# A new issue order for the first five eighths of a one-core attention-and-MoE kernel: same instructions, other places, some on other engines

## The chip, the cores and the metric

The kernel runs on one core of one Trainium2 chip. Such a core has five engines that each take their instructions strictly in order: PE (TensorE, matmuls, with its weight loads shown as PEld), DVE (VectorE), ACT (ScalarE), POOL (GpSimd) and SP (SyncE), which here only issues DMAs. Engines wait for each other by semaphores. The metric is the time of one execution on the device in microseconds (us). For the kernel before, three runs gave 907.27, 907.62 and 909.55 us, median 907.62.

## The reference, cut to what matters

Batch 4, 8 heads, 768 positions, 64 values a head; then a gated feed-forward layer over 3072 tokens, 512 wide, 1536 inside.

```python
q_bucket = sum((q @ proj > 0) * 2**arange(6)); k_bucket likewise
mask = q_bucket[:, :, :, None] == k_bucket[:, :, None, :]
scores = where(mask, q @ k.T / sqrt(64), -1e9)
attn = exp(scores - max);  attn = attn / (sum(attn) + 1e-09)
x = (attn @ v), heads side by side          # 3072 x 512
return ((x @ w_a) * (x @ w_b)) @ w_out      # all in float32
```

## The kernel before

**Tiling.** A batch is cut into 3 chunks of 256 tokens, a chunk's attention into 2 halves of 4 heads, a half into 8 score tiles of 128 queries by 768 keys. So there are 192 score tiles. A tile is named by batch, chunk, half, head pair in the half, head in the pair and token tile: `e_1_2_0_0_1_1` is the exponential of batch 1, chunk 2, half 0, pair 0, head 1, tile 1.

**One score tile** (`qtile`, L1044). PE computes `s` (L1056, with keys `kTA`, `kTB` and queries `qTA`, `qTB`, each transposed, of 16-bit parts and bucket marks). DVE takes the row maximum `mx` (L1070) and a small `width` (L1079); `bias` runs on ACT (L1086) or DVE (L1092). ACT makes `e`, the exponential (L1102). `e` is split into a 16-bit high part (a cast into `a2`, on DVE L1113, ACT L1114 or POOL L1115) and a low part (a subtraction on POOL L1125 or DVE L1129). SP issues a DMA transpose of both, `at` (L1135), and PE multiplies it with the values `vh` and `vl` into `av` (L1144). The first chunk of batch 0 goes another way, by PE transposes (`et`, L1023, and `av`, L1037).

**The feed-forward part** (`moe`, L1325) of a chunk has 12 steps f. PE makes `ab` (L1349, 24 matmuls), ACT scales one half into `a` (L1363), DVE multiplies into `g` (L1371), `g` is split into 16-bit parts (L1379 on ACT or L1383 on DVE; L1391 on POOL), and PE adds `o` (L1401, 6 matmuls). There is one PSUM buffer for `ab`: the `ab` of step f+1 begins only when the `g` of step f has read it. So `a` and `g` stand between each two `ab`.

**Preparing a batch.** For each of the 4 head pairs of a batch SP loads keys (`rk_k`, L737) and values (`vr`, L737), and for each chunk queries (`rq_q`, L952). The first reader of such a load is an absolute maximum or sum: on ACT L754, on DVE L757 (`mx_k`, `mx_v`), for queries L962 or L968. Then come a PE broadcast `ps` (L463), `al` (L469), the scale, the split into the parts `nB` (L886, L890, L907), copies into `marked` (L898, L902), a DMA transpose (L847), the bucket matmuls `b_k`, `b_q` (L819) and their marks (L828, L832). The weights of the feed-forward part are loaded and split during batch 0 (L532 to L665).

**What sets the order.** Every operation is recorded first (`Plan.op`), with the engine it runs on by default and, for the free pieces, with one or two other engines (`alt`). `Plan.issue` then walks over the table `ORDER` (L104 to L300): an entry is the number of an operation, plus 10000 or 20000 where its first or second other engine is taken; a negative entry -n puts n matmuls named `warm` (L1505) on PE, which compute nothing that is used. So the table alone sets what stands behind what on each engine, DMA issues on SP included.

```python
for x in order:
    if x < 0:
        fill(-x)
        continue
    which, at = divmod(x, 10000)
    o = self.ops[at]
    (o.alt[which - 1][2] if which else o.fn)()
```

Of the kernel before, what the change touches and what calls it, by code (L numbers as in the profile page):

```python
# [75 lines left out]
def constants():  # L76
# [28 lines left out]
    2, 7, 1, 4, 6, 13, 5, 0, 53, 61, 41, 8, 280, 254, 276, 10014, 3, 9, 281, 10, 277, 11, 15, 10054, 27, 12, 257,  # L105
    16, 10062, 138, 17, 55, 258, 56, 57, 253, 63, 10018, 42, 64, 19, 65, 59, 43, 20, 44, 256, 21, 392, 67, 46, 391,
    10022, 278, -5, 47, 282, 10295, 283, 23, 10048, 24, 279, -6, 25, 284, 290, 60, 285, 286, 45, 26, 287, 288, 68,
    289, -13, 49, 50, 10028, 291, -6, 51, 294, 259, 10267, 322, 52, 323, 296, 10139, 260, 10272, -13, 29, 326, 255,
    150, 30, 327, 261, 31, -9, 140, 262, 70, 141, 32, 263, 69, 264, 78, 71, 266, 33, 10406, 72, 79, 271, 10073, 80,
    265, 74, 34, 81, -20, 86, 268, 82, 396, 75, 395, 87, 94, 20269, 300, 76, 299, 142, 270, 88, 83, 143, 95, 84,  # L110
    328, 96, 324, 89, 97, -7, 85, 10336, 90, 325, 329, 98, 393, 91, 330, 145, 331, 92, 35, 394, 146, 99, 10151, 273,
    100, 559, 397, 20274, 10036, 304, -7, 152, 398, 303, 153, 275, 332, 399, 154, -7, 400, 37, 401, 155, 333, 38,
    335, 402, -6, 39, 157, 405, 93, 10040, 144, 158, 292, 337, 102, 110, 410, 103, 293, 147, 148, 560, 104, 149,
    10105, 403, 106, 111, 20297, 340, 561, 162, 10318, -16, 107, 112, 306, 368, 118, 113, 305, 313, 10341, 302, 301,
    108, 156, 119, 114, -11, 159, 77, 407, 562, 126, 120, 307, 160, 121, 408, 564, 122, 163, 409, 565, 411, -15,
    308, 115, 309, 127, 101, 116, 161, 128, 179, 310, 129, 342, 317, 123, 412, 130, 373, 180, 134, -9, 187, 20413,
    312, 178, 117, 188, 298, 124, 170, 189, 311, 190, -5, 131, 181, 191, 314, 182, 132, 195, 414, 375, 345, 109,
    183, 196, 133, 315, 334, 184, 197, 10198, 203, 319, 185, 199, 316, 58, 204, 192, 350, 349, 10171, 205, 566,
    10193, 346, 206, 369, 567, 207, 20320, 372, 172, 173, 211, 135, 569, 321, 404, 174, 164, 125, 165, 176, 219,
    166, 646, 168, 200, 136, 20338, 212, 201, 194, 563, 213, 364, 10214, 202, 169, 568, 208, 215, 339, 220, 186,  # L120
    209, 227, 221, 10222, 351, 216, 223, 228, 10359, 210, 217, 235, 229, 230, 177, 224, 231, 819, 10382, 236, 225,
    570, 237, 370, 20343, 232, 10238, 571, 239, 218, 344, 371, 233, 579, 572, 10573, 137, 574, 226, 580, 234, 243,
    575, 581, 588, 10820, 582, 240, 576, 583, 589, 241, 597, 244, 590, 20584, 821, 577, 591, 242, 598, 592, 585,
    599, 245, 600, 606, 601, 374, 20593, 586, 607, 822, -4, 615, 594, 608, 66, 246, 578, 609, 10602, 616, 610, 595,
    603, 247, 10611, -10, 624, 617, 824, 604, 618, 619, 249, 625, 825, 620, -10, 633, 376, 626, 248, 347, 627, 628,
    348, 612, -4, 250, 634, 10629, 377, 596, 635, 378, 10636, 621, 352, 647, 637, 613, 353, 379, 648, 251, 354, 587,
    630, 355, 605, 10638, 649, 622, 10650, 356, 656, 651, 252, 639, 631, 363, 657, -3, 665, 464, 20652, 358, 658,
    10659, 175, 666, 653, 614, 660, 667, 465, 10668, 640, 357, 669, 360, 674, 466, 381, 623, 10823, 467, 683, 654,
    365, 468, 471, 661, 469, 684, 419, 10670, 472, 662, 420, 675, 361, 415, 685, 416, 641, 676, 10686, 473, 10362,
    470, 677, 663, 687, 10671, 678, 826, 632, 474, 20366, 386, 827, 478, 383, 828, 387, 479, 10367, 475, 642, 692,  # L130
    476, 480, 643, 644, 10679, 701, 481, 477, 688, 388, 439, 384, 485, 689, 693, 672, 482, 430, 694, 10695, 486,
    702, 444, 483, 696, 418, 680, 664, 703, 487, 492, 655, 10704, 697, 829, 488, 710, 385, 705, 422, 681, 495, 711,
    489, 435, 443, 712, 496, 10713, 417, 440, 698, 714, 1103, 380, 484, 690, 421, 389, 167, 490, 423, 441, 424, 497,
    830, 390, 425, 10706, 426, 673, 498, 429, 831, 839, 502, 840, 499, 707, 434, 832, 841, 682, 10833, 446, 699,
    834, 503, 500, 427, 10842, 428, 715, 843, 491, 431, 708, 504, 716, 505, 848, 432, 445, 509, 442, 459, 433, 447,
    849, 448, 510, 506, 493, 449, 450, 719, 850, 10494, 857, 851, 507, 511, 523, 691, 835, 436, 501, 717, 852,
    10836, 508, 844, 1079, 20437, 512, 1104, 858, 709, 845, 10853, 866, 859, 1105, 837, 645, 700, 1106, 516, 10860,
    10438, 846, 861, 517, 1108, 513, 454, 514, 867, 875, 1109, 518, 854, 718, 10862, 519, 515, 868, 876, 869, 453,
    863, 720, 855, 877, 527, 721, 520, 10878, 870, 722, 526, 521, 723, 879, 1107, 838, 871, 906, 455, 884, 864,
    11080, 1110, 522, 872, 528, 1111, 456, 529, 1112, 847, 885, 530, 457, 880, 1081, 533, 886, 1082, 10887, 1083,  # L140
# [1403 lines left out]
```

## Time and profile before

| what | value |
|---|---|
| median of three runs | 907.62 us (907.27 to 909.55) |
| the profiled execution | 907.48 us, of which 905.4 us from first to last instruction |
| PE busy, share of the span | 865.2 us, 96% |
| DVE, ACT, POOL busy | 660.1, 539.9, 437.5 us |
| mean granted TensorE clock | 0.997 of full speed |
| DMA queue q1, share of 16 engines' span | 80.2% |

The profiled execution stands 2.08 us above its span and 0.14 us below the median of the runs. Busy PE time includes the `warm` matmuls. In the rows a name's numbers are left out, so `rk_k` is each of the key loads; which one it is follows from the order of the instructions.

### The profile page before, as it was taken

The page shows a single profiled execution, that of the slowest core. Times are in us where ns is not written, and L with a number is a line of the kernel's source. Part 1 is how long each engine was busy: PE and PEld are TensorE (multiplying, and loading weights), DVE is VectorE, ACT ScalarE, POOL GpSimd, SP SyncE. Part 2 cuts the span into 40 slices and gives each one's busy share as a digit, 9 for nine tenths or more (in the row PEclk, how much of TensorE's full clock was granted, in tenths as well). Part 3 has the DMA queues.
Part 4 walks back from the last instruction along what each step waited for, and adds up shares of the span by engine and source line. Part 5 has one row for each costly group of instructions (what it writes and reads, how often), then busy time and mean ns, then how long its engine had stood idle before and what let it go on. Part 6 is the DMA issues. An engine that isn't in the chain of part 4 may idle for free.

```text
span 905.4 us, 23135 instructions
## 1 busy us (share of the span) xinstructions
PE 865.2 (96%) x9252; PEld 661.0 (73%) x9252; DVE 660.1 (73%) x1557; ACT 539.9 (60%) x1043; POOL 437.5 (48%) x384
## 2 busy tenths in 40 slices
PE   4799899999999998999999999999999999999998
PEld 3678687776777776777777777777777777777775
DVE  6999999988778787779767667767888865652210
ACT  6897899967655665465653466545666655452212
POOL 1568868685544454353543264564454544362111
PEclk9999999999999999999999999999999999999999
DMA  8786699999988899989759679998899966744000
GB/s 315 253 225 188 125 238 241 180 194 192 210 179 143 158 175 181 160 168 171 148 126 165 106 151 157 191 173 150 152 188 164 174 110 105 130 94 72 1 24 24
DMA packets 416987, 142.61 MB, mean 158 GB/s; under 512 B 388592, under 2 KB 409200, under 8 KB 416880
## 3 DMA queue, kind: packets, MB, share of 16 engines
q1 hardware_dynamic: 416880, 141.14, 80.2%
q8 instruction: 72, 1.18, 0.5%
q14 instruction: 35, 0.29, 0.1%
HBM read 37.82 MB, written 6.29 MB: 49 GB/s over the span
## 4 chain that ended last, share of the span: by engine, by line
PE 70%; DVE 15%; DMA 6%; ACT 3%; issue 3%; SPq 2%; POOL 1%; ACTq 0%; DVEq 0%; POOLq 0%
PE ab L1349 34%; PE o L1401 16%; PE s L1056 10%; PE av L1144 7%; DMA at<-a 3%; DVE mx L1070 3%; PE av L1037 2%; DMA rq_q<-in_q_dram 1%; ACT e L1102 1%; DVE g L1371 1%; DVE wmx L637 1%; DVE nB_q L907 1%; DMA rk_k<-in_k_dram 1%; DVE wab L576 1%; DVE width L1079 1%
## 5 line engine op out<-in xcount | busy, mean ns | idle before, releaser
L1349 PE MATMUL ab<-xT,wab 128*128 128x256 f16 x3456 | 409.2, 273 | 7.5 <-DVE g L1371 7.3
L1349 PEld LDWEIGHTS <-wab 128*128 128x128 f16 x3456 | 333.5, 98 | 61.3 <-issue 8.9
L1125 POOL TENSOR_TENSOR a<-e,a 128x768 f16<-128x768 f32 x129 | 217.9, 1691 | 124.4 <-ACT a L1114 59.2
L1102 ACT ACTIVATE e<-s,bias,width 128x768 f32<-128x768 f32 x192 | 189.8, 989 | 82.3 <-DVE bias L1092 68.1
L1391 POOL TENSOR_TENSOR g<-g,g 128x256 f16<-128x256 f32 x144 | 103.7, 720 | 228.1 <-ACT g L1379 144.8
L1070 DVE TENSOR_REDUCE mx<-s 128x1 f32<-128x768 f32 x192 | 182.0, 950 | 38.9 <-PE s L1056 38.0
L1401 PE MATMUL o<-wo,g 128*128 128x512 f16 x864 | 209.0, 379 | 0.0
L1371 DVE SCALAR_TENSOR_TENSOR g<-ab,wlow,a 128x256 f32<-128x256 f32 x132 | 63.5, 481 | 105.6 <-ACT a L1363 98.2
L1401 PEld LDWEIGHTS <-g 128*128 128x128 f16 x864 | 81.3, 98 | 74.3
L1363 ACT ACTIVATE a<-ab,wcut 128x256 f32<-128x256 f32 x144 | 67.6, 469 | 110.3 <-PE ab L1349 108.4
L1144 PEld LDWEIGHTS <-at 128*128 128x128 f16 x3168 | 112.1, 98 | 22.3 <-DMA at<-a 4.6
L1144 PE MATMUL av<-vh,at 128*128 128x64 f16 x2112 | 115.4, 193 | 2.4 <-DMA at<-a 2.4
L1056 PE MATMUL s<-kTA_k,qTA_q 128*128 128x384 f16 x384 | 93.8, 326 | 5.6 <-ACT e L1102 3.5
L1056 PE MATMUL s<-kTB_k,qTB_q 128*128 128x384 f16 x384 | 93.8, 326 | 0.0
L1115 POOL CAST a<-e 128x768 f16<-128x768 f32 x52 | 44.5, 857 | 62.8 <-ACT e L1102 42.6
L1114 ACT CAST a<-e 128x768 f16<-128x768 f32 x83 | 68.6, 830 | 2.5 <-DMA at<-a 1.0
L1379 ACT CAST g<-g 128x256 f16<-128x256 f32 x103 | 41.4, 402 | 45.6 <-DVE g L1371 38.0
L1086 ACT ACTIVATE bias<-mx,width 128x1 f32<-128x1 f32 x91 | 26.4, 292 | 69.8 <-DVE width L1079 69.4
L1144 PE MATMUL av<-vl,at 128*128 128x64 f16 x1056 | 59.6, 193 | 0.0
L1056 PEld LDWEIGHTS <-qTB_q 128*128 128x128 f16 x384 | 37.5, 98 | 24.9
L1129 DVE TENSOR_TENSOR a<-e,a 128x768 f16<-128x768 f32 x47 | 47.0, 1002 | 8.4 <-ACT a L1114 6.6
L1056 PEld LDWEIGHTS <-qTA_q 128*128 128x128 f16 x384 | 34.8, 99 | 23.4 <-issue 5.9
(156 smaller groups left out, 871.7 us busy)
## 6 DMA issues: line engine op xcount, KB each, us to landing
rk_k<-in_k_dram SPq DMA_DIRECT2D x16, 384.0 KB, 4.4
vr<-in_v_dram SPq DMA_DIRECT2D x16, 384.0 KB, 4.3
rq_q<-in_q_dram SPq DMA_DIRECT2D x12, 512.0 KB, 4.7
raw_w<-in_moe_w_b_dram SPq DMA_DIRECT2D x12, 512.0 KB, 6.8
raw_w<-in_moe_w_a_dram SPq DMA_DIRECT2D x12, 512.0 KB, 6.4
raw_wo<-in_moe_w_out_dram SPq DMA_DIRECT2D x12, 512.0 KB, 5.7
out_dram<-ob SPq DMA_DIRECT2D x24, 256.0 KB, 2.8
at<-a SPq DMA_TRANSPOSE x176, 4.1
```

What stands on the lines that cost most here:

```text
L1056: nc.tensor.matmul(ps.t[:, jj, :HALF], lhsT=x.t[:, uq, :], rhs=y.t[:, h * NT + jj * 3 : h * NT + jj * 3 + 3, :].rearrange("p t x -> p (t x)"),
L1070: lambda: nc.vector.tensor_reduce(out=mx.t[:, u : u + 1], in_=halves(ps.t), axis=AX.XY, op=ALU.max, negate=True),
L1102: lambda: nc.scalar.activation(flat2(e.t), halves(ps.t), AF.Exp, bias=bias.t[:, u : u + 1], scale=width.t[:, u : u + 1], accum_out=sm.t[:, ...
L1114: ("ACT", 0.725, lambda: nc.scalar.copy(out=a2.t[:, 0], in_=e.t), False),
L1125: lambda: nc.gpsimd.tensor_tensor(out=a2.t[:, 1], in0=e.t, in1=a2.t[:, 0], op=ALU.subtract),
L1129: lambda: nc.vector.tensor_tensor(out=a2.t[:, 1], in0=e.t, in1=a2.t[:, 0], op=ALU.subtract), True,
L1144: nc.tensor.matmul(av.t[:, u, :], lhsT=at.t[:, a + kt, :], rhs=w.t[:, h, kt, :], start=i == 0, stop=i == 3 * NT - 1,)
L1349: nc.tensor.matmul(pl.t[:, m, :CH], lhsT=wt(m, wi, cc, f), rhs=xt.t[:, :, xi * NC + cc, :], start=i == 0, stop=i == 3 * NC - 1,)
L1363: lambda a=a, pl=pl, gr=gr: nc.scalar.activation(a.t, pl.t[:, 0, :CH], AF.Copy, scale=wcut[:, gr : gr + 1]),
L1371: lambda a=a, g32=g32, pl=pl, cut=cut: nc.vector.scalar_tensor_tensor(out=g32.t, in0=pl.t[:, 1, :CH], scalar=cut, in1=a.t, op0=ALU.mult, o ...
L1391: lambda g=g, g32=g32: nc.gpsimd.tensor_tensor(out=g[1].t, in0=g32.t, in1=g[0].t, op=ALU.subtract),
L1401: nc.tensor.matmul(po.t[:, u, :], lhsT=g[gi].t[:, us], rhs=wo[f // 2].t[:, f % 2, wi * DM : (wi + 1) * DM], start=f % per_q == 0 and i == ...
```

## The change

Only the table `ORDER` differs. Both tables hold the same 3658 operations. 198 of them run on another of their engines than before, and the negative entries (the `warm` matmuls) add up to 207 instead of 186. From the `ab` of batch 1, chunk 2, step 9 on, PE has the same sequence as before to the end; the other engines join within a few instructions of it. Over the whole program the casts of `e` are now 33 on DVE, 77 on ACT and 66 on POOL (41, 83 and 52 before). A line of the table from its start and one from the middle:

```diff
@@ -102,201 +102,201 @@
 ORDER = [
-    2, 7, 1, 4, 6, 13, 5, 0, 53, 61, 41, 8, 280, 254, 276, 10014, 3, 9, 281, 10, 277, 11, 15, 10054, 27, 12, 257,
...
-    1075, 11693, 11964, 1699, 1694, 1076, 1338, 1700, 1335, 1077, 1577, 21695, 1337, 1701, 1965, 1702, 1078, 1703,
...
+    2, 6, 7, 1, 5, 13, 4, 0, 53, 61, 41, 8, 254, 276, 281, 14, 9, 280, 10, 277, 15, 11, 10054, 258, 16, 257, 17, 27,
...
+    1964, 1939, 1719, 1337, 11720, 11077, 1335, 1721, 1965, 1569, 11966, 1339, 1336, 1706, 1340, 1580, 1968, 1341,
...
```

On DVE, in batch 1, chunk 2, ahead of the `g` of feed-forward step 5 of chunk 0 (`g_1_0_5`), these stood before; `rk_k2_1` is the key load of batch 2, pair 1:

```order
L907 SCALAR_TENSOR_TENSOR nB_k2_0_5758<-rk_k2_0_94,ks_k2_0_5940,nB_k2_0_5758 128x12x64
L1092 TENSOR_SCALAR bias_1_2_0_5524<-mx_1_2_0_5482,width_1_2_0_5519 128x1
L902 COPY marked_79<-nB_k2_0_5758 128x12x64
L757 TENSOR_REDUCE mx_k2_1_6034<-rk_k2_1_95 128x1
L1371 SCALAR_TENSOR_TENSOR g_1_0_5_6054<-ab_1_0_5_5967,wlow_76,a_1_0_5_6023 128x256
L1383 TENSOR_REDUCE g0_1_0_5_6060<-g_1_0_5_6054 128x256
```

Now these stand on DVE ahead of the same `g`:

```order
L1070 TENSOR_REDUCE mx_1_2_1_6008<-s_1_2_1_0_0_0_5981 128x1
L1079 TENSOR_SCALAR width_1_2_1_6025<-mx_1_2_1_6008,qsig_q1_2_4608 128x1
L1092 TENSOR_SCALAR bias_1_2_1_6027<-mx_1_2_1_6008,width_1_2_1_6025 128x1
L1070 TENSOR_REDUCE mx_1_2_1_6008<-s_1_2_1_0_0_1_6001 128x1
L1113 CAST a2_1_2_1_0_0_0_6065<-e_1_2_1_0_0_0_6030 128x768
L1079 TENSOR_SCALAR width_1_2_1_6025<-mx_1_2_1_6008,qsig_q1_2_4608 128x1
L1129 TENSOR_TENSOR a2_1_2_1_0_0_0_6065<-e_1_2_1_0_0_0_6030,a2_1_2_1_0_0_0_6065 128x768
L1371 SCALAR_TENSOR_TENSOR g_1_0_5_6080<-ab_1_0_5_6012,wlow_76,a_1_0_5_6075 128x256
```

The maximum over `rk_k2_1` has left DVE; it is now an L754 on ACT, behind `e_1_2_1_0_1_0`, and two score tiles of the next half have moved ahead of this `g`.

On ACT, a little earlier, the first reader of the key load of batch 2, pair 0 (`rk_k2_0`) stood like this, between the `a` of steps 2 and 3:

```order
L1363 ACTIVATE a_1_0_2_5706<-ab_1_0_2_5652,wcut_73 128x256
L1102 ACTIVATE e_1_2_0_0_1_1_5714,sm_1_2_0_5534<-s_1_2_0_0_1_1_5641,bias_1_2_0_5524,width_1_2_0_5519 128x768
L1379 CAST g0_1_0_2_5729<-g_1_0_2_5720 128x256
L1114 CAST a2_1_2_0_0_1_1_5732<-e_1_2_0_0_1_1_5714 128x768
L754 ACTIVATE nB_k2_0_5758,mx_k2_0_5759<-rk_k2_0_94 128x12x64
L1240 ACTIVATE xz_1_1_1_5778<-x_1_1_0_5276,xsc_1_1_5749 128x256
L1240 ACTIVATE xz_1_1_1_5778<-x_1_1_1_5716,xsc_1_1_5749 128x256
L1363 ACTIVATE a_1_0_3_5799<-ab_1_0_3_5734,wcut_73 128x256
```

And now, between the same two `a`:

```order
L1363 ACTIVATE a_1_0_2_5772<-ab_1_0_2_5695,wcut_73 128x256
L1379 CAST g0_1_0_2_5792<-g_1_0_2_5781 128x256
L1102 ACTIVATE e_1_2_0_1_0_1_5794,sm_1_2_0_5501<-s_1_2_0_1_0_1_5685,bias_1_2_0_5494,width_1_2_0_5492 128x768
L1086 ACTIVATE bias_1_2_0_5494<-mx_1_2_0_5478,width_1_2_0_5492 128x1
L1102 ACTIVATE e_1_2_0_1_1_0_5828,sm_1_2_0_5501<-s_1_2_0_1_1_0_5774,bias_1_2_0_5494,width_1_2_0_5492 128x768
L754 ACTIVATE nB_k2_0_5861,mx_k2_0_5862<-rk_k2_0_94 128x12x64
L1363 ACTIVATE a_1_0_3_5873<-ab_1_0_3_5799,wcut_73 128x256
```

The reader now stands behind the exponential of a tile three further on, with two exponentials and a bias between the `a` of step 2 and it; on SP the load's issue stands behind the transpose `at_1_2_0_0_0_0` as before and has moved ahead of the transpose `qTB_q2_0`.

On SP in batch 0, chunk 2, the key load of batch 1, pair 0 (`rk_k1_0`) stood like this:

```order
L1135 DMA_TRANSPOSE at_0_1_1_1_1_1_2260<-a2_0_1_1_1_1_1_2144 128x12x128
L737 DMA rk_k1_0_87<-in_k_dram 128x2x384
L1135 DMA_TRANSPOSE at_0_2_0_0_0_0_2313<-a2_0_2_0_0_0_0_2249 128x12x128
L1135 DMA_TRANSPOSE at_0_2_0_0_0_1_2351<-a2_0_2_0_0_0_1_2271 128x12x128
L847 DMA_TRANSPOSE qTB_q1_0_2379<-nB_q1_0_2278 128x16x128
L1135 DMA_TRANSPOSE at_0_2_0_0_1_0_2418<-a2_0_2_0_0_1_0_2301 128x12x128
```

And now:

```order
L1135 DMA_TRANSPOSE at_0_1_1_1_1_1_2250<-a2_0_1_1_1_1_1_2159 128x12x128
L1135 DMA_TRANSPOSE at_0_2_0_0_0_0_2317<-a2_0_2_0_0_0_0_2252 128x12x128
L1135 DMA_TRANSPOSE at_0_2_0_0_0_1_2370<-a2_0_2_0_0_0_1_2262 128x12x128
L847 DMA_TRANSPOSE qTB_q1_0_2394<-nB_q1_0_2272 128x16x128
L737 DMA rk_k1_0_87<-in_k_dram 128x2x384
L1135 DMA_TRANSPOSE at_0_2_0_0_1_0_2437<-a2_0_2_0_0_1_0_2344 128x12x128
```

The load has moved behind three transposes; its reader on ACT stands behind the same exponential, `e_0_2_0_1_0_1`, as before.

## Rows read from the trace of the kernel before

**Rows 1.** The page's first part: busy us, share of the span, instructions.

```profile
PE 865.2 (96%) x9252; PEld 661.0 (73%) x9252; DVE 660.1 (73%) x1557; ACT 539.9 (60%) x1043; POOL 437.5 (48%) x384
```

**Rows 2.** Windows: stretch, its us, each engine's busy us, clock, DMA share, GB/s.

```profile
20.00:112.00 92.00, 80.15 (x765) 65.98 (x764) 86.83 (x217) 78.98 (x125) 64.19 (x43) 1.00 0.74 204
112.00:200.00 88.00, 86.29 (x1015) 65.91 (x1015) 83.59 (x205) 80.49 (x145) 64.57 (x48) 1.00 1.12 214
200.00:507.60 307.60, 301.10 (x3304) 227.37 (x3302) 240.16 (x566) 173.62 (x356) 136.35 (x124) 0.99 0.90 166
507.60:880.00 372.40, 368.70 (x3960) 281.23 (x3959) 235.19 (x530) 189.23 (x393) 164.94 (x155) 1.00 0.72 127
```

**Rows 3.** Waits of PE: us in total, times, longest us.

```profile
PE ab L1349 <- DVE g L1371: 7.3, 7, 2.6
```

**Rows 4.** Timeline 340 to 350 us: start, us, engine, line, operation [idle before, releaser].

```profile
340.23 0.57 SPq L737 DMA_DIRECT2D rk_k<-in_k_dram  x1
...
341.15 2.78 PE L1349 MATMUL ab<-xT,wab 128*128 128x256 f16 x24
...
344.77 0.84 ACT L754 ACTIVATE nB_k<-rk_k 128x768 bf16<-128x768 f32 x1 [3.11 <-DMA rk_k<-in_k_dram]
...
346.41 0.45 ACT L1363 ACTIVATE a<-ab,wcut 128x256 f32<-128x256 f32 x1
...
346.97 0.48 DVE L1371 SCALAR_TENSOR_TENSOR g<-ab,wlow,a 128x256 f32<-128x256 f32 x1 [2.56 <-ACT a L1363]
...
347.51 1.47 PE L1349 MATMUL ab<-xT,wab 128*128 128x256 f16 x12 [1.36 <-DVE g L1371]
```

**Rows 5.** Timeline 357 to 364 us.

```profile
358.07 0.57 SPq L737 DMA_DIRECT2D rk_k<-in_k_dram  x1
...
361.82 0.95 DVE L757 TENSOR_REDUCE mx_k<-rk_k 128x1 f32<-128x768 f32 x1 [3.45 <-DMA rk_k<-in_k_dram]
362.69 0.47 DVE L1371 SCALAR_TENSOR_TENSOR g<-ab,wlow,a 128x256 f32<-128x256 f32 x1
```

**Rows 6.** Timeline of PE, 357 to 372 us.

```profile
363.22 4.45 PE L1349 MATMUL ab<-xT,wab 128*128 128x256 f16 x24 [2.55 <-DVE g L1371]
```

**Rows 7.** Windows, the ten us around that wait.

```profile
360.00:370.00 10.00, 7.45 (x72) 5.31 (x71) 5.65 (x11) 4.70 (x10) 4.37 (x5) 0.83 1.06 192
```

**Rows 8.** Timeline of PE, 192 to 196 us.

```profile
194.31 0.50 PE L1056 MATMUL s<-kTA_k,qTA_q 128*128 128x384 f16 x2 [1.17 <-DMA kTA_k<-marked]
```

**Rows 9.** Timeline 206 to 210 us.

```profile
206.99 1.64 POOL L1125 TENSOR_TENSOR a<-e,a 128x768 f16<-128x768 f32 x1
207.06 2.38 DVE L1129 TENSOR_TENSOR a<-e,a 128x768 f16<-128x768 f32 x1 [1.51 <-DMA rk_k<-in_k_dram]
...
208.39 0.35 PE L1144 MATMUL av<-vh,at 128*128 128x64 f16 x6 [0.83 <-DMA at<-a]
```

**Rows 10.** Timeline 488 to 500 us.

```profile
489.30 0.56 DVE L1113 CAST a<-e 128x768 f16<-128x768 f32 x1 [3.02 <-DMA at<-a]
...
497.91 2.34 PE L1349 MATMUL ab<-xT,wab 128*128 128x256 f16 x20 [0.78 <-DVE g L1371]
```

**Rows 11.** Timeline 150 to 164 us, SP and ACT.

```profile
150.71 0.57 SPq L737 DMA_DIRECT2D rk_k<-in_k_dram  x1
...
155.69 1.36 SPq L847 DMA_TRANSPOSE qTB_q<-nB_q  x1
...
161.40 0.84 ACT L754 ACTIVATE nB_k<-rk_k 128x768 bf16<-128x768 f32 x1 [0.43 <-DMA qTB_q<-nB_q]
```

**Rows 12.** Groups by line: busy us, mean ns of one, idle before.

```profile
L1129 DVE TENSOR_TENSOR a<-e,a 128x768 f16<-128x768 f32 x47 | 47.0, 1002 | 8.4 <-ACT a L1114 6.6 <-DMA rk_k<-in_k_dram 1.5
L1115 POOL CAST a<-e 128x768 f16<-128x768 f32 x52 | 44.5, 857 | 62.8 <-ACT e L1102 42.6 <-DMA at<-a 15.6 <-PE b_k L819 3.4
...
L1505 PE MATMUL warm<-ident 128*128 128x256 f16 x186 | 24.9, 281 | 0.0
```

**Rows 13.** Waits of DVE, 0 to 120 us: us in total, times, longest.

```profile
DVE mx L1070 <- PE s L1056: 2.3, 4, 0.9
DVE al_proj L469 <- PE ps_proj L463: 2.2, 1, 2.2
```

386 rows, old and new, of the table ORDER are left out of this document.

## The prediction

> **What bounds the kernel now.** I read the first part of the page, then busy time by stretches, then the waits of PE, and last the timeline around each wait. PE is busy for 865.2 of 905.4 us, 96%; DVE is next with 73% [rows 1]. So the end is set by PE: its busy time, plus the stretches where it stands. The difference between a stretch and PE's busy time in it tells where it stands [rows 2]: 11.85 us from 20 to 112, 1.71 from 112 to 200, 6.5 from 200 to 507.6, 3.7 from 507.6 to 880. The first 20 and the last 25.4 us hold the rest: 40.2 - 23.76 = 16.4. The `warm` matmuls are 24.9 us of the busy time [rows 12], and in the order all of them stand ahead of the first `ab` of batch 0, at some 112 us; so 20 to 112 us hold some 37 us in which PE has nothing useful to do, the largest reserve of this kernel.
>
> From batch 1, chunk 2, step 9 on, the edge of the stretches at 507.6 us, PE's sequence is unchanged, so whatever the change gains or loses has to happen before 507.6 us: in the start stage, or in the 1.71 + 6.5 = 8.2 us between 112 and 507.6. Most of these 8.2 us lie at six places, and I read what released PE at each.
>
> **Places that may be mended.** *First:* at 340.23 SP issues the key load of batch 2, pair 0; ACT stands 3.11 us for it and reads it only at 344.77, 4.54 us after the issue [rows 4]. The `a` of the feed-forward step is queued behind that reader, comes at 346.41, `g` at 346.97, and `ab` on PE begins at 347.51 after 1.36 us idle. In the changed order the reader stands behind an exponential three tiles further on, and the issue is a transpose earlier on SP. With tiles of 905.4 / 192 = 4.7 us, the reader gets several us more than the 3.11 it waited. I take the 1.36 as gone (bounds 0 and -1.36).
>
> *Second:* the load of pair 1 is issued at 358.07, and its reader, on DVE, waits 3.45 us and runs at 361.82; `g` stands directly behind it, at 362.69 [rows 5]. PE waits 2.55 us for it, and the `ab` behind that takes 4.45 us for 24 matmuls [rows 6], against 2.78 for the same 24 at 341.15 [rows 4]. The granted clock of 360 to 370 us is 0.83 [rows 7]: behind the 2.55 us of idle PE ran for a while at the lower level, 1.2 GHz, and that cost 4.45 - 2.78 = 1.67. The place is worth 2.55 + 1.67 = 4.22 us, the dearest of the middle. In the changed order the reader has left DVE and stands on ACT three tiles later. I take all 4.22 (bounds 0, where the late landing only meets ACT instead, and -4.22).
>
> *Third:* 1.17 us before the first `s` of batch 1 at 194.31, which waits for the transposed keys [rows 8]. In the changed order about 0.9 us more of PE's own work stands between the bucket matmuls of that pair and this `s`, by the groups of matmuls that the order lists there. I take -0.9 (0 to -1.17).
>
> *Fourth:* 0.83 us at 208.39, where `av` waits for `at` [rows 9]. The subtraction that makes its low part took 2.38 us on DVE against a mean of 1.00 for the line [rows 12], beside a POOL subtraction from 206.99. The reader of the key load of that place has moved from ACT to DVE, behind `g`; the landing may be covered or not. Half: -0.4 (0 to -0.83).
>
> *Fifth:* 0.78 us at 497.91 behind a cast on DVE that stood 3.02 us for the transpose that still read its buffer [rows 10]. The engines of the casts are shuffled there; -0.6 (0 to -0.78).
>
> Sum of what can be mended: -4.22 - 1.36 - 0.9 - 0.4 - 0.6 = -7.5, of the 8.2 us that are there.
>
> The fourth place is also where a rule speaks against the change. By the Trainium skill, "SBUF — State Buffer", section "Who interferes with whom", an instruction of DVE that reads two SBUF inputs and one of GpSimd exclude each other, since they share one port pair, for as long as an instruction lasts. The 2.38 us beside a POOL subtraction agree with it [rows 9]; the other runs of that line, 1.00 us in the mean [rows 12], with POOL busy in nearly half the span, don't show it as a steady cost. By the rule the 14 casts that move to POOL could hold up DVE; that is a rival below.
>
> **What the change adds.** *Spacing of `ab`.* `a` and `g` stand between two `ab`: from `a` at 346.41 to the next `ab` is 1.10 us [rows 4] at best. By the order, 25 places now have under 2 us of other PE work between two `ab` (16 before), the tightest one tile's `s` and `av`, about 1.2 us. The seven waits of `ab` for `g` sum to 7.3 us before, of which the three above are 4.69 [rows 3, 4, 6, 10]; the other 2.6 over 13 tight places are 0.2 each. Nine more places would then cost 1.8; some of them have DVE and ACT free ahead, so I take +0.85 (0 to 1.8).
>
> *The load of batch 1, pair 0* has moved behind three transposes on SP, the last of which, `qTB`, is issued 4.98 us later than the load was (155.69 against 150.71), while the reader stays behind the same exponential and ran at 161.40, after 0.43 us for the transpose's landing [rows 11]. Issued just behind it, at 157.05, and landing 4.54 us later as in [rows 4], the load is there at 161.6: 0.2 later than the reader ran before. I take +0.6, since the transposes share the DMA engines (bounds 0 and 4.22, the price of the worst such place).
>
> *The start.* DVE gets a `mx_k` (0.95 as in [rows 5]), two `bias` and a cast of 0.56 [rows 10] ahead of the first feed-forward inputs, and gives up a step of the split. The longest wait of DVE there is 2.2 us for one broadcast matmul, beside 2.3 in four small ones [rows 13]; the added work can fill that. I take +0.3; the bounds are -2.3 (all of the four waits gone) and +2.2 (a wait of the longest kind more).
>
> *21 more `warm` matmuls* cost nothing where they stand in waits, as nearly all do before 112 us; if all of them came on the path, 21 x 24.9 / 186 = 2.8 us [rows 12]. I take +0.4 (0 to 2.8).
>
> *New readers on DVE:* those of pairs 1 and 2 of batch 1 and pair 2 of batch 2, which were on ACT. Each runs 0.95 instead of 0.84, which is hidden with DVE at 240 of 307.6 us in that stretch [rows 2]. If its load is late, it holds the `g` behind it exactly as in [rows 5]: 0 to +4.22 each. I take 0: in the order all three stand one to three instructions behind a `g`, so that most of a feed-forward step lies before the next.
>
> Sum of the additions: 0.85 + 0.6 + 0.3 + 0.4 = +2.15. Together -7.5 + 2.15 = -5.3, and 907.48 - 5.3 = 902.2 us for an execution like the profiled one, which lies 0.14 under the median of the runs. So I predict 902.2.
>
> **The rivals.**
>
> *A, the idle time moves and does not go.* What removes a stall here lets PE run ahead until it meets the next late thing: more work of the same DVE (83.59 of 88.00 us busy from 112 to 200 [rows 2]) or another landing. There DVE, and not PE's own waits, sets the pace, and POOL's additional casts don't relieve it unless they are what DVE drops. For it: in that stretch DVE stands under 5%. Against: from 200 to 507.6 DVE has 67 us free, and the two dear places are single late landings, with no shortage of an engine behind them. By it only the clock loss and part of one gap go, -1.67 - 1.36 + 2.15 = about -0.9: 906.6. Chance 0.2.
>
> *B, a load lands late before a DVE reader.* The mechanism of [rows 5 to 7], now at two of the three readers that moved to DVE: the wait decides once it is longer than PE's work between the two `ab` (from 2 us on at many places), and a gap over 2.5 us brings the half clock with it. Price 2 x 4.22 = 8.4, on top of 902.2: 910.6, slower. For it: each of these readers is a first reader of a load, which is what DVE stood 3.45 us for. Against: on ACT these same readers stood in places without a gap on PE of that size, and DVE reaches them behind a `g`. Chance 0.11.
>
> *C, the casts on POOL block DVE.* 14 casts of 0.857 us [rows 12] that each hold up a two-input instruction of DVE on the path cost 12.0 us: 902.2 + 12.0 = 914.2. For it the 2.38 us of [rows 9]; against it the mean of 1.00 of that line. This is the rule of the Trainium skill named above, taken at its strongest. Chance 0.02.
>
> That the change doesn't do what it says is excluded: the readers and issues stand in other places in the order.
>
> **How the numbers follow.** The forecast has the remaining 0.67. Its own range is 898.5, where the starting stage gives 2.3 instead of costing 0.3 and the `ab` spacing costs nothing, to 904.9, where half of the 5.3 is not had. A difference under 0.3%, 2.7 us, can't be told from none: faster means under 904.9, slower over 910.3. The cases give faster 0.67, same 0.2, slower 0.13. The range leaves out B, C and a bit at the bottom: 898.5 to 908.5.
>
> **What would show it.** Right: the idle before the `ab` of batch 1, chunk 0, steps 4 and 6 is under 0.3 us, the granted clock of that ten us is 1.00, and the first feed-forward `ab` of batch 0 begins within a us of where it did. The first `s` of batch 1 waits under 0.4. Rival A: these gaps are gone, but PE's idle time from 112 to the joining place is still over 7 us, in other places. Rival B: a wait of over 2 us on DVE for a key load, a gap of PE behind it and a clock under 1 in that stretch. C: the mean of L1129 on DVE well over 1.00. Wrong altogether: a new stretch of PE idle that none of these names, above all before 112 us, where over 30 us are to be had or lost by changes that I priced at +0.3.

## The result and the profile after

The changed kernel takes 898.77 us (median of 4 runs, 897.19 to 900.57) against 907.44 us beside it: ratio 0.9903, 95% interval 0.9875 to 0.9932, faster by 8.7 us. Run once more with the experiments it took 898.19 us, ratio 0.9905 (0.9883 to 0.9926). Forecast were 902.2 and faster; the first median lies in the range (898.5 to 908.5) by 0.3 us, the second 0.3 us below it, and the gain is 1.6 times the forecast.

The first part of the page, answering to [rows 1] (busy us, share, instructions):

```profile
PE 863.4 (96%) x9273; PEld 662.1 (74%) x9273; DVE 644.3 (72%) x1544; ACT 535.1 (60%) x1040; POOL 448.2 (50%) x399
```

POOL has 10.7 us more to do, DVE 15.8 us less; PE is busy for 1.8 us less, so 8.2 of the 10.0 us that this execution's span is shorter are idle time of PE. The waits of PE, answering to [rows 3] (us in total, times, longest):

```profile
PE ab L1349 <- DVE g L1371: 2.3, 4, 0.8
...
PE s L1056 <- DMA qTA_q<-marked: 1.0, 1, 1.0
```

`ab` waits 2.3 us for `g` instead of 7.3, never over 0.8; a wait for the transposed queries has come. To see where, I cut the span at the starts of the same matmuls in each trace: the first `ab` of batch 0 chunk 0 (step 0), of batch 0 chunk 2 (step 6) and of batch 1 chunk 2 (step 9, the joining place), and of the last step of all. The rows are windows: stretch, its us, busy time of PE, PEld, DVE, ACT, POOL, clock, DMA share, GB/s. First the kernel before:

```profile
112.97:285.41 172.44, 169.66 (x1953) 128.79 (x1952) 150.25 (x376) 130.17 (x247) 105.51 (x85) 1.00 1.05 199
285.41:507.56 222.15, 217.04 (x2362) 164.07 (x2360) 172.48 (x394) 122.97 (x252) 94.40 (x87) 0.99 0.87 160
507.56:894.31 386.75, 383.05 (x4062) 291.22 (x4061) 237.11 (x534) 191.86 (x399) 167.66 (x159) 1.00 0.70 122
```

The kernel before in a second trace, taken with the experiments:

```profile
113.28:285.61 172.33, 169.31 (x1954) 128.71 (x1953) 152.01 (x376) 130.55 (x247) 104.24 (x85) 1.00 1.05 199
285.61:506.48 220.87, 216.87 (x2361) 163.99 (x2360) 172.19 (x394) 123.04 (x252) 94.55 (x87) 0.99 0.88 161
506.48:892.75 386.27, 383.05 (x4061) 291.20 (x4060) 237.06 (x534) 191.87 (x399) 167.66 (x159) 1.00 0.68 122
```

The changed kernel:

```profile
113.61:285.01 171.40, 169.93 (x1958) 129.54 (x1956) 146.79 (x371) 127.63 (x244) 102.40 (x86) 1.00 1.05 202
285.01:499.16 214.15, 214.01 (x2358) 162.64 (x2356) 161.28 (x385) 121.44 (x256) 109.80 (x103) 1.00 0.90 166
499.16:884.35 385.19, 382.93 (x4062) 291.29 (x4061) 235.70 (x531) 191.22 (x399) 166.73 (x158) 1.00 0.67 123
```

Its second trace, the middle stretch:

```profile
285.44:499.58 214.14, 214.01 (x2357) 162.64 (x2356) 161.14 (x385) 121.30 (x256) 109.68 (x103) 1.00 0.90 166
```

Read the first two columns. The second stretch goes from 222.15 and 220.87 us to 214.15 and 214.14, 6.7 to 8.0 us, and PE is now idle in it for 0.14 us. In the first stretch the difference is 0.5 to 1 us. But the cut between the two doesn't split the same work: the changed order runs the four matmuls `s` of one more score tile ahead of it. Windows of the second stretch for the tile `s` alone, PE's busy time and count, before and changed:

```profile
285.41:507.56 222.15, 40.50 (x204) 0.99 0.87 160
285.01:499.16 214.15, 40.03 (x200) 1.00 0.90 166
```

Four such matmuls take 0.65 us of PE: in the kernel before, those ahead of the `ab` at 341.15 [rows 4] begin at 340.50. Like for like the second stretch gains 6.1 to 7.4 us, most of the whole, and the first 1.2 to 1.7. The third has the same order on PE in both kernels. Most of the 0.7 to 1.6 us there is one `av` near 765 us, which waits 1.23 and 1.27 us before and 0.27 and 0.56 in the changed kernel. It waits 1.24 and 1.59 us in two experiments that have the changed order ahead of the joining place (new from 280, late on ACT), so this part doesn't follow from the change. Another 0.3 us lies outside the span: the time stands 2.1 us above the span in the runs of the kernel before and 1.8 in those of the changed one; why is not known.

At the two dear places, answering to [rows 4] and [rows 5] (timeline of SP, ACT, DVE and PE; start, us):

```profile
332.01 0.87 SPq L737 DMA_DIRECT2D rk_k<-in_k_dram  x1
...
344.29 0.83 ACT L754 ACTIVATE nB_k<-rk_k 128x768 bf16<-128x768 f32 x1
...
345.64 0.47 ACT L1363 ACTIVATE a<-ab,wcut 128x256 f32<-128x256 f32 x1 [0.43 <-PE ab L1349]
...
345.84 0.88 SPq L737 DMA_DIRECT2D rk_k<-in_k_dram  x1
...
346.56 0.48 DVE L1371 SCALAR_TENSOR_TENSOR g<-ab,wlow,a 128x256 f32<-128x256 f32 x1
...
348.37 0.82 PE L1349 MATMUL ab<-xT,wab 128*128 128x256 f16 x6
...
364.52 0.83 ACT L754 ACTIVATE nB_k<-rk_k 128x768 bf16<-128x768 f32 x1
```

The loads are issued 12.3 and 18.7 us ahead of their readers (4.54 and 3.75 before), and neither reader has a bracket: nothing is waited for. `a` now waits for PE, not for a load. The ten us that answer to [rows 7] have PE busy throughout, at full clock:

```profile
360.00:370.00 10.00, 10.00 (x128) 7.57 (x126) 6.91 (x20) 5.63 (x13) 5.00 (x5) 1.00 1.09 237
```

The key load of batch 1, pair 0, that moved behind three transposes, answering to [rows 11]:

```profile
155.87 3.54 SPq L847 DMA_TRANSPOSE qTB_q<-nB_q  x1
...
159.46 0.57 SPq L737 DMA_DIRECT2D rk_k<-in_k_dram  x1
...
163.52 0.87 ACT L754 ACTIVATE nB_k<-rk_k 128x768 bf16<-128x768 f32 x1
```

The reader runs 4.06 us after the issue and waits for nothing. The new wait is elsewhere, at the first `s` of batch 0, chunk 2 (timeline of PE):

```profile
139.75 0.50 PE L1056 MATMUL s<-kTA_k,qTA_q 128*128 128x384 f16 x2 [0.98 <-DMA qTA_q<-marked]
```

Ahead of it on SP (timeline of SP, issues and how long each holds the queue):

```profile
127.79 3.33 SPq L1135 DMA_TRANSPOSE at<-a  x1
131.22 0.53 SPq L532 DMA_DIRECT2D raw_wo<-in_moe_w_out_dram  x1
131.84 4.35 SPq L847 DMA_TRANSPOSE qTA_q<-marked  x1
```

### The profile page after: what moved, and what is told of

Same layout as the page of the kernel before. It is cut to its first block, busy times and chain, and to the rows that moved or that the text cites. A ratio compares the mean times of both kernels' runs of the same rounds, so it can differ in the third digit from the quotient of the medians.

```text
span 895.4 us, 23179 instructions
## 1 busy us (share of the span) xinstructions
PE 863.4 (96%) x9273; PEld 662.1 (74%) x9273; DVE 644.3 (72%) x1544; ACT 535.1 (60%) x1040; POOL 448.2 (50%) x399
## 4 chain that ended last, share of the span: by engine, by line
PE 77%; DVE 5%; DMA 2%; ACT 1%; issue 1%; ACTq 0%; DVEq 0%; SPq 0%
PE ab L1349 38%; PE o L1401 19%; PE s L1056 11%; PE av L1144 9%; DVE mx L1070 1%; DMA qTA_q<-marked 1%; DMA rq_q<-in_q_dram 1%; DVE g L1371 1%; DVE xz L1251 1%; DMA at<-a 0%; PE b_k L819 0%; PE b_q L819 0%; DVE nB_q L907 0%; ACT e L1102 0%; DVE width L1079 0%
## 5 line engine op out<-in xcount | busy, mean ns | idle before, releaser
L1115 POOL CAST a<-e 128x768 f16<-128x768 f32 x66 | 56.0, 851 | 46.9 <-ACT e L1102 35.9
L1086 ACT ACTIVATE bias<-mx,width 128x1 f32<-128x1 f32 x97 | 28.5, 294 | 72.4 <-DVE width L1079 72.1
L1114 ACT CAST a<-e 128x768 f16<-128x768 f32 x77 | 63.9, 831 | 2.7 <-DMA at<-a 1.4
L1056 PEld LDWEIGHTS <-qTB_q 128*128 128x128 f16 x384 | 37.5, 98 | 24.9
L1129 DVE TENSOR_TENSOR a<-e,a 128x768 f16<-128x768 f32 x46 | 45.5, 993 | 6.0 <-ACT a L1114 5.8
```

The lines of the kernel that those rows point to most:

```text
L1056: nc.tensor.matmul(ps.t[:, jj, :HALF], lhsT=x.t[:, uq, :], rhs=y.t[:, h * NT + jj * 3 : h * NT + jj * 3 + 3, :].rearrange("p t x -> p (t x)"),
L1114: ("ACT", 0.725, lambda: nc.scalar.copy(out=a2.t[:, 0], in_=e.t), False),
L1115: ("POOL", 0.9, lambda: nc.gpsimd.tensor_copy(out=a2.t[:, 0], in_=e.t), False),
```

## The experiments

Theory: a few first readers of loads stood ahead of `a` and `g` and came before their data; put later than the landing, they give back the gaps and what hangs on them. Rivals: the idle time only moves; or the gain comes from the engines of the pieces (POOL relieves DVE). All times are of five rounds with the kernel before beside them. The last three columns are the stretches above, from each kernel's trace; in experiments the lines stand 7 or 8 further down, since their tables have more lines.

| kernel | median us | ratio to before (95%) | start to first `ab` | 1st | 2nd | 3rd |
|---|---|---|---|---|---|---|
| before, two traces | 907.2 to 907.9 | 1 | 112.97, 113.28 | 172.44, 172.33 | 222.15, 220.87 | 386.75, 386.27 |
| changed, two traces | 898.2 | 0.9905 (0.9883 to 0.9926) | 113.61, 113.65 | 171.40, 171.79 | 214.15, 214.14 | 385.19, 385.56 |
| two readers | 902.79 | 0.9948 (0.9930 to 0.9965) | 113.67 | 172.47 | 215.55 | 386.49 |
| new from 280 | 901.89 | 0.9944 (0.9922 to 0.9967) | 116.08 | 171.27 | 214.13 | 386.63 |
| new to 280 | 905.56 | 0.9980 (0.9966 to 0.9995) | 113.77 | 171.62 | 219.29 | 385.52 |
| late on ACT | 904.28 | 0.9969 (0.9956 to 0.9983) | 114.49 | 172.72 | 218.37 | 386.66 |
| late on DVE | 900.70 | 0.9929 (0.9908 to 0.9949) | 114.78 | 173.31 | 214.15 | 385.10 |
| pieces back | 902.81 | 0.9956 (0.9933 to 0.9979) | 115.19 | 173.75 | 216.42 | 385.48 |
| pieces alone | 908.89 | 1.0013 (0.9992 to 1.0035) | 113.34 | 172.44 | 219.54 | 387.18 |
| readers and pieces | 905.08 | 0.9967 (0.9948 to 0.9987) | 115.11 | 172.52 | 216.92 | 387.55 |
| four waits removed | 900.33 | 0.9919 (0.9896 to 0.9943) | 116.27 | 172.06 | 214.15 | 385.70 |
| the same, mended | 897.64 | 0.9896 (0.9869 to 0.9924) | 113.24 | 171.53 | 214.14 | 385.86 |

The start is the first lesson of the table: it differs by up to 3.1 us between traces of kernels that have one and the same order in it (112.97 to 116.08 in the order before), and the third stretch, which has one order on PE in all kernels but the last two, runs from 385.10 to 387.55. Two traces of the very same kernel differ by 0.31 us at most in the start, and the times of the kernel before by 9.6 us (902.58 to 912.19); whether it is the execution or the program that moves the start is not shown. So the time of one run tells less than its stretches do.

To compare the first two stretches across the table, mind the tile that crosses the cut: the two traces of the changed kernel, new from 280, late on ACT, late on DVE, pieces back and the last two rows have its `s` in the first stretch, the others in the second. For those, 0.65 us belongs off the first column and onto the second.

**Two readers.** The order before with two entries moved behind the `a` and the `g` that they held up:

```diff
-    1583, 11940, 1352, 1349, 1715, 1727, 1584, 1723, 1970, 1353, 1728,
+    1583, 1352, 1349, 1715, 1727, 1584, 1723, 1970, 1353, 11940, 1728,
...
-    1776, 1952, 1725, 1368, 21758, 1973, 11369, 1373,
+    1776, 1725, 1368, 21758, 1973, 11369, 1952, 1373,
```

> The order before, with two entries moved and nothing else: the first reader of the key load of batch 2, pair 0, goes on ACT from ahead of `a` of step 3 to right behind it, and the reader of pair 1 goes on DVE from ahead of `g` of step 5 to right behind it. Theory (late landings: a reader that waits for its load holds up the `a` or `g` queued behind it): the two gaps on PE go (1.36 and 2.55 us), with the half clock behind the second (1.7 to 1.8) and the slower first matmuls behind a gap (0.16 each): -5.9 us, 901.5. Rival (idle time moves and does not go): the readers' chains come a step later, new gaps open in the next steps, and the whole is -2 us or less, 905.5 to 907.5.

902.79 us, a ratio that means 3 to 6 us under before; the theory's 901.5 lies within that, the rival's 905.5 does not. Its timeline at the first place (`ab` of step 3, `a`, the reader, the next `ab`):

```profile
341.88 2.78 PE L1356 MATMUL ab<-xT,wab 128*128 128x256 f16 x24
...
344.70 0.47 ACT L1370 ACTIVATE a<-ab,wcut 128x256 f32<-128x256 f32 x1 [0.86 <-PE ab L1356]
345.07 0.83 ACT L761 ACTIVATE nB_k<-rk_k 128x768 bf16<-128x768 f32 x1
...
346.71 1.48 PE L1356 MATMUL ab<-xT,wab 128*128 128x256 f16 x12
```

`a` begins 2.8 us after the `ab` that it reads, against 5.3 before, and the next `ab` has no bracket. At the second place the reader still stands 0.42 us for its load, now behind `g`, and holds up nothing. The second stretch falls to 215.55, so two entries give 5.3 to 6.6 of the 6.1 to 7.4 us of that stretch, all but 0.75. That one place later is enough, with the loads left where they were, is the strongest sign for the theory; a gap of 0.46 us at step 7 is what the rival can claim.

**The table in two halves.** At 280 us the two tables have done the same operations but for two, so that they can be joined there.

> The order before up to about 280 us (1300 of the 3658 operations), the changed order for the rest; at this point the two tables have done the same operations but for two. Theory: nearly all of the gain sits here, in named gaps: 1.36 + 2.55 + 1.7 (half clock) + 0.78 + 0.35 (two small ones) and 0.16 for each restart, -7.5 us: 900. Rival (the gain is spread, since the engines around PE are less loaded everywhere): half of the gain, since it is half of the changed stretch: -4.3 us, 903.

> The reverse: the changed order up to about 280 us, the order before for the rest. Theory: +0.6 in the start stage, -1.17 -0.83 and some small gaps, +0.99 for a new wait of the first `s` of chunk 2, about -1 to -2.4 us: 905 to 906.4; the two gaps behind the key loads of batch 2 stay as they were. Rival (spread gain): -4.3 us, 903.

```diff
-ORDER = [ the table before ]
+ORDER = [ its first 1300 operations, then the rest in the changed order ]
...
+ORDER = [ the first 1298 in the changed order, then the rest in the order before ]
```

901.89 and 905.56 us. The first of these, by itself, speaks for the rival: its interval, 900.1 to 904.2, holds the rival's 903 and not the theory's 900. The stretches tell why: the second half has the 214.13 us of the changed kernel, and from the first `ab` to the last step the trace takes 772.03 us, against 770.74 and 771.49 of the changed kernel and 781.34 and 779.48 before; what is missing is the start, 116.08. The other kernel has the changed first half, with 171.62 in the first stretch. But the order before, entered from there, takes 219.29 instead of 221 to 222, with gaps of 0.75 and 1.92 us where 1.36 and 2.55 stood, and a new one of 1.14 at step 4 of the next chunk. So halves do not add up exactly; why the gaps shrank was not tried. The spread-gain rival (903 each) fails by the stretches and by the 905.56, whose interval (904.1 to 906.8) is clear of 903.

> The changed kernel once more, beside the three others. Both theories: 898.8 us, ratio 0.990. The stretch behind 507 us has the same order in all of these kernels: what differs there between their traces is what one execution differs from another.

898.19 us, as expected; the traces agree to 0.4 us in each stretch.

**Late again.** The changed kernel with only the issue of loads moved back, first two whose readers are now on ACT, then one whose reader has moved to DVE (1724, 1760 and 977 are transposes `at` on SP):

```diff
 late on ACT
-    1964, 1939, 1719,
+    1724, 1939, 1582,
-    1716, 1951, 1942,
+    1760, 1951, 1787,
 late on DVE
-    743, 1206, 979,
+    977, 1206, 1140,
```

> The changed kernel with only two load issues on SP moved later: the key loads of batch 2, pairs 0 and 1, are issued behind the transposes `at_1_2_0_0_1_1` and `at_1_2_0_1_1_1`, about 11 and 17 us later, so that their readers, at their new places on ACT, come before the landing again. Theory (it is the landing, not the engine or the place, that costs): each reader waits 2 to 3.5 us, the `a` behind it is late, PE stands 1 to 2.5 us at each: +2 to +6 us against the changed kernel, 901 to 905. Rival (the changed order has slack for it): +1 or less.

> The changed kernel with one load issue moved: the key load of batch 1, pair 2, is issued behind the transpose `at_0_2_1_1_1_1`, some 6 us later. Its reader is one of those that moved to DVE. It should stand there some 3 us. Theory, with the price of my slower rival: the stall on DVE passes PE's work between two `ab` and costs 2 to 4.2 us: 901 to 903. Rival: PE's lead over DVE covers it, +0.5 or less, 899.

904.28 and 900.70 us: 6.1 and 2.5 us over the changed kernel. The rival's 1 and 0.5 us are out; against the theory the first time lies in its range (901 to 905), the second 0.3 under (901 to 903). In the stretches where the edits act the price is smaller: 4.2 us (218.37 against 214.15) and 1.5 to 1.9 (173.31 against 171.79 and 171.40); the rest lies in stretches that the edits don't reach. The trace shows a way that I had not seen. On ACT (load, reader, PE; then PE at the second load, where the reader of the values stands directly behind the late one on ACT):

```profile
345.28 0.62 SPq L744 DMA_DIRECT2D rk_k<-in_k_dram  x1
...
349.41 0.84 ACT L761 ACTIVATE nB_k<-rk_k 128x768 bf16<-128x768 f32 x1 [2.83 <-DMA rk_k<-in_k_dram]
...
350.40 0.23 PE L470 MATMUL ps_k<-ident,mx_k 128*128 128x128 bf16 x1 [1.95 <-ACT nB_k L761]
...
373.25 0.23 PE L470 MATMUL ps_v<-ident,mx_v 128*128 128x128 bf16 x1 [1.02 <-ACT vh L761]
```

and on DVE:

```profile
207.87 0.58 SPq L744 DMA_DIRECT2D rk_k<-in_k_dram  x1
...
211.65 0.95 DVE L764 TENSOR_REDUCE mx_k<-rk_k 128x1 f32<-128x768 f32 x1 [1.90 <-DMA rk_k<-in_k_dram]
...
212.66 0.23 PE L470 MATMUL ps_k<-ident,mx_k 128*128 128x128 bf16 x1 [1.54 <-DVE mx_k L764]
```

PE does not stand for `g`: it stands for the reader itself, in a broadcast matmul of 0.23 us that waits in PE's own queue ahead of `ab`. So a late load has two ways to PE, and in the changed order the second is the shorter. A stall of 1.90 us on DVE cost 1.54 on PE: my rival B had the late landing before a DVE reader right, led it to PE through `g` and not through the broadcast, and priced it at 4.22 for each.

**The engines of the pieces.** 50 pieces of the split of `e` set back to the old engines in the changed order, then the reverse in the order before, then the reverse with the two readers:

```diff
 pieces back: 50 entries of the changed table, for example
-    21740, 11758, 11772,
+    11740, 21758, 1772,
 pieces alone: the same 50 in the table before
-    11740, 21758, 1772,
+    21740, 11758, 11772,
```

> The changed kernel with the engine of each piece of the split of `e` (cast or subtraction) set back to that of the kernel before, 50 of them, at the same places of the table: 27 of them leave POOL, 13 come to it. Theory (late landings): the engines of these pieces are secondary: +0 to +1.5 us, up to 900.3. Rival (POOL relieves DVE, and that is the gain): +4 us or more, 903.

902.81 us: 4.6 over the changed kernel, the rival's number and not the theory's (900.3 at most). Gaps open at several places, the largest where [rows 9] had one:

```profile
208.91 0.35 PE L1151 MATMUL av<-vh,at 128*128 128x64 f16 x6 [1.09 <-DMA at<-a]
```

> The order before, with the engine of each of the same 50 pieces of the split of `e` as in the changed kernel, and no entry moved. If relief of DVE (POOL takes 14 casts more) is a gain of its own, worth what taking it back cost the changed kernel: -4.5 us, 902.7. If the engines only help together with the new order (late landings theory): -1.5 to +1.5 us, 906 to 909, with the gaps behind the key loads of batch 2 as before.

> The order before with the two readers one place later and the engines of the 50 pieces as in the changed kernel: the two ingredients that have shown an effect, and nothing else of the new order. If the two account for the gain: -4.5 - 4.5 = -9 us, 898.5. If the engines help only in the new order: as with the readers alone, -4.5 us, 902.5 to 903.

908.89 us, no gain, and 905.08, not better than the readers alone. So relief of DVE is not a gain of its own: the engines belong to the places, and each order needs its own. Two readers and 50 engines together don't make up the rest of the gain. Between the two readers alone and the changed kernel, like for like, 0.75 us of it lies in the second stretch and 1.3 to 1.7 in the first, where the order as a whole differs; I can't name a single entry for that. Some 1 us lies in the third stretch and 0.3 outside the span.

**Waits of the changed kernel removed.** Four edits of the same sort, and then two more. 10823 and 828 are the copy into `marked` and the transpose for the queries of batch 0, chunk 2; 12824 is the maximum over a query load, 2445 and 2708 make `xz`, 2926 and 12927 are the load of `rk_k3_2` and its reader, 443 is a weight load, 2276 an output store; 481, 2214, 2242 and 2523 are `g`, 2466 is an `a`:

```diff
 four waits removed
-    486, 10823, 483,
-    10695, 828, 421,
+    430, 10823, 828, 481,
-    2550, 12824, 2213,
+    2214, 12824, 2411,
-    12591, 2445, 2832,
+    2242, 2445, 2592,
-    2958, 2708, 2876,
+    2523, 2708, 2883,
 the same, mended: further
+    827, 10823, 476,
+    10367, 828, 443,
+    2658, 2926, 2276,
+    2466, 12927, 2669,
```

> The changed kernel with four waits of its own trace taken away in the same manner: on DVE the copy into `marked` for the queries of batch 0, chunk 2, one step earlier, ahead of `g`, with its transpose; the maximum over the query load of batch 3, chunk 0, behind the `g` that it held up; two multiplications of `xz` behind the `g` of steps 2_0_7 and 2_1_10. Theory: 0.99 + 0.43 + 0.76 + 0.80 and 0.16 for each restart, -3.6 us: 895.2. Rival (idle time moves): -1 or less, 898.

900.33 us: no gain, 5 us over the theory and 2 over the rival's own number. Its start is 2.6 us longer; from the first `ab` to the last step the trace takes 771.91 us against 770.74 and 771.49. That is the rival's case: three gaps ahead of `ab` went (0.43, 0.76 and 0.80), two of 0.40 and 0.32 came ahead of `s`, and another landing came late behind them (reader, `a`, `g`, `ab`):

```profile
603.47 0.84 ACT L761 ACTIVATE nB_k<-rk_k 128x768 bf16<-128x768 f32 x1 [4.74 <-DMA rk_k<-in_k_dram]
...
604.31 0.46 ACT L1370 ACTIVATE a<-ab,wcut 128x256 f32<-128x256 f32 x1
...
604.87 0.48 DVE L1378 SCALAR_TENSOR_TENSOR g<-ab,wlow,a 128x256 f32<-128x256 f32 x1 [3.48 <-ACT a L1370]
...
605.41 0.82 PE L1356 MATMUL ab<-xT,wab 128*128 128x256 f16 x6 [0.83 <-DVE g L1378]
```

And the first edit gave nothing (the first `s` of that chunk waits 1.48 us): the copy was early, but on SP the transpose stayed behind a weight load that was itself behind a long transpose. Its releaser was SP's queue, not the data.

> The kernel before once more, for a second trace of it. Theory (late landings): the gaps ahead of `ab` of steps 4 and 6 stand again, within 0.5 us, and the stretch from 280 us to the joining place takes the 222 us of the first trace; where it is shorter, the half clock is missing. The start stage, in the same order, may differ by 1 to 3 us between the two traces. The time is that of before, ratio 1.000.

908.12 us, ratio 1.0005. The gap of step 6 stands again (2.60), that of step 4 is 0.95 instead of 1.36; in the first stretch the two gaps of [rows 8] and [rows 9] are replaced by 1.30 and 0.78 us at other places, at the same length of the stretch.

> The version with four waits removed, with the late landing that took their place mended too: the load of the keys of batch 3, pair 2, is issued ahead of two output stores, and its reader on ACT goes behind the `a` that it held up; and the transpose of the queries of batch 0, chunk 2, goes ahead of the weight load that SP issued before it. Theory: -0.83 for the gap of batch 2, chunk 1, step 3, and about -0.5 for the first `s` of chunk 2: 1.3 to 2 us under the version with four edits, 898.5 or less, and 1 to 3 us under the changed kernel from the start of `ab` on. Rival (idle time moves): another landing is late behind it, no gain, 900.

897.64 us, the fastest median of all, 10 us under before; but its interval (0.9869 to 0.9924) covers that of the changed kernel, and from the first `ab` on its trace is not shorter (771.53 against 770.74 and 771.49 us, the sums of three stretches). A gain over the changed kernel is not shown.

## Why the prediction was right, and where it was off

**The second place** (-4.22) went as written: gap and half clock are gone. The second trace of before has it at 2.60 + 4.24 - 2.78 = 4.06, and the `o` behind it takes 1.71 us instead of 1.46, so the half clock cost 1.7 us there too.

**The first place** (-1.36) went, and two entries show that it was the reader; in the second trace it is worth 0.95.

**Third, fourth and fifth** (-1.9 of 2.78): all three gaps are gone from the changed kernel, so the halves I left were too careful; but in the first stretch the order before has such gaps at changing places, and the net there, like for like, is only 172.4 to 170.9, -1.4, with the new 0.98 for the transposed queries among it. I had looked for a stall behind SP's transposes at the key load and not at the query transposes, where it came.

**The additions** (+2.15) came to about the sum, but as other terms. `ab` spacing: one gap of 0.35 us between 112 and 507 us, not 0.85. The working was wrong here: it laid the 2.6 us of waits of `ab` that were left, 0.2 each, on 13 tight places of the changed part. But 2.4 of them stand behind the joining place, where nothing changed. The waits of PE in the kernel before, 112 to 507 us and from 507 on:

```profile
PE ab L1349 <- DVE g L1371: 4.9, 4, 2.6
...
PE ab L1349 <- DVE g L1371: 2.4, 3, 0.9
```

Of the 4.9 the three named places are 4.69, so the 13 tight places cost 0.2 together. The load past three transposes: 0, not 0.6; it landed within 4.06 us though a transpose of 3.54 us was issued ahead of it. Start and `warm`: +0.64 and +0.37 between pairs of traces, inside the 3.1 us by which starts of one order differ; `warm` costs nothing that can be seen. With the new wait of 0.98, which no term had, this makes some 1.7 us.

**What made the gain larger** is thus mostly what was mended, not the additions. Like for like the second stretch gives 6.7 us in the mean of two traces, where the first, second and fifth place were priced at 6.2; the first stretch gives 1.4, where the terms of its own came to about nothing (-0.9 and -0.4 against +0.6 and a part of the 0.85). Less 0.5 at the start that is 7.6 us, against 5.3 forecast. The other 1.4 us of these traces, 1.1 behind the joining place and 0.3 outside the span, lie where I had said that nothing could be gained, and it is they that took the time to the edge of the range. So the direction and the two dear places were right by their mechanism; that the additions came near their sum was luck.

**Slips of the working that don't move the forecast.** The 7.5 us to be mended are not all "of the 8.2 us that are there": 8.2 is idle time of PE, and 1.67 of the 7.5 is PE busy at half clock. Of the six places only five are named. And 3.0 of the 24.9 us of `warm` lie in the first 20 us, so 20 to 112 us hold 34 us without useful work, not 37.

**New readers on DVE** were priced at 0, which held; there are four of them, since that of batch 1, pair 3, has moved too and I missed it. The changed order lays 7.4 us between issue (200.85) and reading (208.30) of the one I tested, and taking that lead away costs 1.5 to 1.9 us in its stretch.

**Rival A** (idle time moves) was wrong for this change and right for my own next one. The second stretch has 0.14 us of idle time left, so nothing came in place of the two dear gaps. **Rival C** did not come: L1129 on DVE has 993 ns in the mean against 1002 [rows 12], with 14 more casts on POOL.

What stays open is the first stretch, and 0.75 us of the second: the two readers alone account for 4.4 of 8.7 to 9.0 us in the medians, and for 5.3 to 6.6 of 6.1 to 7.4 in the stretch where they stand. The remainder needs the order around them and its choice of engines (taking the engines back cost 4.6), and no experiment here separates it further.

## What to carry to other kernels

Where an engine stands for a load ahead of a short operation that the bounding engine waits for, put the reader behind that operation: here two entries gave half of the gain, at the price of one new gap of 0.46 us. Look for every queue that the wait passes through, the bounding engine's own small matmuls and the issuing engine's queue included. Once few gaps are left, removing one more moves it; judge such edits by the same stretch in several traces, not by one time.

## What the runs showed of the hardware

**The clock.** The same wait of PE had two outcomes. Behind 2.60 us idle the second trace of before had a granted clock of 0.83 in the ten us around it; behind 2.61 us the kernel with the pieces alone stayed at 1.00 and its 24 matmuls took 2.78 us, not 4.24. The `ab` behind the gap in the one and in the other (its lines stand 8 further down):

```profile
363.07 4.24 PE L1349 MATMUL ab<-xT,wab 128*128 128x256 f16 x24 [2.60 <-DVE g L1371]
...
362.74 2.78 PE L1357 MATMUL ab<-xT,wab 128*128 128x256 f16 x24 [2.61 <-DVE g L1379]
```

Windows ahead of and around the gap, of the second trace of before:

```profile
350.00:360.00 10.00, 9.86 (x104) 6.90 (x103) 8.00 (x21) 6.11 (x13) 4.15 (x5) 1.00 1.12 181
360.00:370.00 10.00, 7.41 (x76) 5.21 (x72) 5.57 (x11) 4.68 (x10) 4.37 (x5) 0.83 1.04 186
```

The same of the kernel with the pieces alone:

```profile
350.00:360.00 10.00, 10.00 (x114) 7.22 (x112) 7.56 (x19) 6.57 (x14) 5.85 (x6) 1.00 1.08 180
360.00:370.00 10.00, 7.39 (x91) 5.88 (x88) 8.05 (x15) 4.16 (x9) 3.09 (x4) 1.00 1.15 214
```

What the rows of PE show to differ is the ten us ahead: it paused for 0.14 us in the one and not at all in the other. Whether that decided it was not tried. So the 1.7 us of half clock are no fixed part of a gap of this length, and rival B's "a gap over 2.5 us brings the half clock with it" does not hold as a rule.

**DVE beside POOL.** The multiplication of `xz` (L1251, two inputs in SBUF besides its scale) has a median of 477 ns and a maximum of 1876 in the changed kernel:

```profile
L1251 DVE SCALAR_TENSOR_TENSOR xz<-x,xsc,xz x40: 465/477/1876, 170.0 to 763.5; 128x256 f16<-128x256 f32 x40
```

The slow ones stand where POOL runs a subtraction (timeline of DVE in the changed kernel):

```profile
560.56 2.26 DVE L1251 SCALAR_TENSOR_TENSOR xz<-x,xsc,xz 128x256 f16<-128x256 f32 x2
```

POOL at that time:

```profile
560.73 1.81 POOL L1125 TENSOR_TENSOR a<-e,a 128x768 f16<-128x768 f32 x1 [2.22 <-DVE a L1113]
```

And PE, whose `ab` waits for the `g` behind them:

```profile
563.27 0.93 PE L1349 MATMUL ab<-xT,wab 128*128 128x256 f16 x7 [0.76 <-DVE g L1371]
```

The pair takes 2.26 us instead of 0.95 and ends 0.3 us after POOL's: its first instruction, begun before POOL's, took 0.48 us, its second, begun after, 1.87. By the Trainium skill, "SBUF — State Buffer", section "Who interferes with whom", a DVE instruction with two SBUF inputs contends with a GpSimd instruction that reads SBUF, and the port pair that they share is an exclusive lock; this trace agrees, at single places (the mean of the line is 585 ns), and not as a cost of every cast on POOL.
